# A fixed instruction sequence for every engine in a kernel that mixes a long convolution and a gated linear unit

## The chip, the cores and the metric

The kernel runs on one core of a Trainium2 chip. A core has four compute engines that run their own instruction queues strictly in order: TensorE (PE, with its weight loads shown as PEld), VectorE (DVE), ScalarE (ACT) and GpSimd (POOL). SyncE (SP) issues nearly all of this kernel's DMAs, also in order. Engines wait for each other through semaphores, so an instruction whose input is late holds up everything behind it on its own engine. The metric is the device time of one execution in microseconds; lower is better.

## What is computed

Two branches work on the same input `u` (2048 positions, 448 channels) and are mixed by a gate per position. All is in 32-bit floats. Cut to what matters:

```python
def _A_ref(u, log_A_real, A_imag, C_real, C_imag, log_dt, D_skip):
    dt = jnp.exp(log_dt)
    A = -jnp.exp(log_A_real) + 1j * A_imag            # 448 x 256
    C = (C_real + 1j * C_imag) * dt[:, None]
    P = jnp.exp((A * dt[:, None])[:, :, None] * pos[None, None, :])
    K = 2.0 * jnp.einsum("dn,dnl->dl", C, P).real     # a filter of 2048 taps per channel
    y = irfft(rfft(u_t, 2 * L) * rfft(K, 2 * L))[:, :, :L]
    return y + u * D_skip

def _B_ref(x, w_gate, w_up, w_down):
    return (sigmoid(x @ w_gate) * (x @ w_up)) @ w_down   # 448 -> 1792 -> 448

g = sigmoid((x * gate_w).sum(-1, keepdims=True))
return g * a + (1 - g) * b
```

## The kernel before

The program is written as a list of operations: each names its engine, a cost, what it reads and writes, and a priority. The class `Plan` turns the list into one order for each engine (`Plan.order`, from L457) and then emits the instructions in that order (`Plan.emit`). The order is worked out while the program is built; on the chip each engine just runs its own fixed list. To find the order, the planner keeps a clock per engine (`Clock`, L350 to L422), takes the engine that could start something first, and among the operations that could start by then picks the one with the smallest priority. The priorities are the numbers of the table `RANK`: for each kind of operation (engine, tile, stage) up to eight numbers, spread over the operations of that kind. The clock counts 450 ns for each DMA that SP issues, whatever its shape, and then 1000 ns, the transfer itself and 550 ns until it has landed.

The work falls into these parts.

- **Constants and parameters** (`step_sizes`, `params`, L926 to L1075; tiles named `..._pro`). Small VectorE chains turn the step sizes and the complex parameters of A and C into two tables in DRAM, `phd` (phases) and `bsd` (powers of the decays). `params` runs once for each half of the channels. Two constant tables are loaded by GpSimd through its own DMA queue (`cast`, L617), which rounds them on the way: `idn`, a 128x128 identity, and `pos`, 96x1024 position patterns.
- **Kernel generation** (`kgen`, 28 chunks of 16 channels, each in two halves, so 56 half chunks). GpSimd multiplies out a table of powers (`tb`, L1105 to L1118). For each half chunk PE makes two 128x512 turn tiles (`turns`, L1128), ScalarE rounds them (L1138, L1139), PE subtracts the rounded part by a matmul with the identity (L1141), ScalarE takes sine and cosine (L1143, L1144, L1158), VectorE makes outer products of the powers (L1165) and multiplies them in (L1179 to L1185), and PE contracts the result to filter taps (L1191, 64 matmuls a half chunk). ScalarE puts the taps into the tile `ke` (L1215). After 14 chunks `ke` goes to DRAM as `kd0`, after 28 as `kd1`; the last VectorE step of each is the addition at L1219.
- **Four transforms** (`Chain`): two for the halves of the input (stage 30 in the tables, stored to `us`), one for each half of the filter (stages 40 and 41). A chain loads its tile `fx`, does a first matmul stage (`stage1_four`, L716), a transposition (through DRAM as `shf`, or on VectorE), a second stage (L749); the filter chains then multiply with `us` (L783), transform back (L793, L830) and add into the output (L834). All input chains and the first filter chain use one and the same tile `fx_fu`, so the next chain's loads wait until the last chain's stores have landed.
- **The gated linear unit** (`glu_up`, `glu_down`). A product is split into rounded and remainder parts, so that a 448-long contraction takes eleven matmuls of 128x512 in four units (`glu_mm`, L1296 to L1301); the way down takes three of 128x448 a step (L1313 to L1315). There are 448 units of the first kind and 224 of the second. Rounding is done by ScalarE (L1244, L1270, L1287), remainders by VectorE (L1248 to L1251, L1272, L1288). The input tile `xs` of 512 positions is loaded and rounded in quarters: two halves of the positions times two halves of the contraction.

Of the PE's work, the gated linear unit depends on nothing but loads and rounding, and the planner spreads it between the steps of kernel generation and the transforms.

## Time and profile before

| | |
|---|---|
| median of 3 runs | 741.96 us (739.8 to 743.25) |
| the profiled execution | 740.59 us, of which the span of the trace is 738.8 us |
| granted TensorE clock, mean | 0.979 |
| kernel generation on VectorE | from 112.3 us (first L1165) to 544 us, with its end at L1219 at 557 us |
| DMAs issued by SP | 379, of which 276.9 us are spent issuing |

How to read what follows. Times in rows are microseconds from the start of the span unless marked ns. A row of the windows shows the busy time of each engine in a stretch, with the number of instructions in brackets, then the granted clock, the DMA share and GB/s. A row of the waits names who waited for whom, with the total, the number of times and the longest. In the chain of waits and the timeline a row starts with its start and its length; a bracket at the end of a timeline row is the idle time of the engine just ahead of it and what ended it. SPq is SP issuing a DMA. A matmul record is about twice as long as the distance to the next one, since matmuls overlap.

### The profile page before, as it was taken

What the parts mean: (1) busy time and instruction counts of PE and PEld (TensorE: products, weight loads), DVE (VectorE), ACT (ScalarE), POOL (GpSimd) and SP (SyncE); (2) the same over time, 40 slices, a digit from 0 to 9 for tenths busy, and PEclk for the clock granted to TensorE, in tenths of its full rate; (3) what the DMA queues carried; (4) which work ended last, traced back from release to release, by engine and by line L of the source; (5) the groups of instructions that cost most, each with busy time, mean ns of one, the idle gap of its engine ahead of it and who ended that gap; (6) DMA issues with size and microseconds to landing.
All of it is one profiled execution on the core that took longest, in us unless ns stands there. A gap on an engine that the chain in (4) does not pass through costs nothing.

```text
span 738.8 us, 16536 instructions
## 1 busy us (share of the span) xinstructions
PE 688.4 (93%) x6628; PEld 498.6 (67%) x6628; DVE 637.9 (86%) x847; ACT 523.7 (71%) x962; POOL 232.7 (32%) x282
## 2 busy tenths in 40 slices
PE   4999899999999999978998899999999899999996
PEld 3788777677757776745666677777778566445863
DVE  6999998999999979999898779999995259775976
ACT  5578749999899779998998789999882342233110
POOL 0043446563455435434543324654400000000000
PEclk9999999999999999988999899999999999999998
DMA  9658337925949945469797913239516963787975
GB/s 291 200 122 217 108 79 203 239 91 171 202 121 223 219 107 160 171 175 204 183 232 180 220 45 125 86 133 175 119 40 131 271 226 100 249 304 207 168 191 142
DMA packets 98660, 126.12 MB, mean 171 GB/s; under 512 B 31224, under 2 KB 81080, under 8 KB 97560
## 3 DMA queue, kind: packets, MB, share of 16 engines
q1 hardware_dynamic: 98328, 124.61, 65.0%
q8 instruction: 52, 0.85, 0.5%
q0 software_dynamic: 256, 0.46, 0.3%
q14 instruction: 24, 0.20, 0.1%
HBM read 81.46 MB, written 43.58 MB: 169 GB/s over the span
## 4 chain that ended last, share of the span: by engine, by line
PE 42%; DVE 19%; ACT 16%; DMA 14%; issue 5%; SPq 3%; POOL 2%; ACTq 0%; DVEq 0%
PE kp_egp L1191 4%; PE gu_gps L1296 4%; PE dn_gps L1313 4%; PE gu_gps L1297 4%; PE gu_gps L1298 4%; PE dn_gps L1314 3%; PE dn_gps L1315 3%; DMA fx_fu<-shf 3%; SPq L615 3%; DVE es_eg L1165 2%; PE tp_egp L1128 2%; PE tp_egp L1141 2%; ACT nn_eg L1139 2%; DMA us<-fx_fu 2%; PE fps_fups L716 2%
## 5 line engine op out<-in xcount | busy, mean ns | idle before, releaser
L1296 PE MATMUL gu_gps<-xs_glu,wh_glu 128*128 128x512 f32 x336 | 138.1, 411 | 16.5 <-ACT wh_glu L1270 10.1
L1298 PE MATMUL gu_gps<-xs_glu,wl_glu 128*128 128x512 f32 x336 | 133.2, 397 | 0.4 <-DVE wl_glu L1272 0.4
L1297 PE MATMUL gu_gps<-xs_glu,wh_glu 128*128 128x512 f32 x336 | 133.3, 397 | 0.0
L1165 DVE TENSOR_TENSOR es_eg<-tb_eg 128x1024 f32<-128x1024 f32 x112 | 107.4, 988 | 7.0 <-POOL tb_eg L1115 3.7
L1313 PE MATMUL dn_gps<-vh_glu,hh_glu 128*128 128x448 f32 x224 | 87.9, 393 | 2.8 <-DVE ob_glu L1329 2.6
L1296 PEld LDWEIGHTS gu_gps<-xs_glu,wh_glu 128*128 128x128 f32 x336 | 64.1, 191 | 39.2 <-ACT wh_glu L1270 10.1
L1115 POOL TENSOR_TENSOR tb_eg<-tb_eg 128x96 f32<-128x96 f32 (+2 forms) x84 | 82.2, 982 | 6.2
L1314 PE MATMUL dn_gps<-vh_glu,hl_glu 128*128 128x448 f32 x224 | 82.6, 369 | 0.6 <-issue 0.4
L1315 PE MATMUL dn_gps<-vl_glu,hh_glu 128*128 128x448 f32 x224 | 82.3, 368 | 0.0
L1139 ACT ACTIVATE nn_eg<-fr_eg 128x512 fp32r<-128x512 f32 x112 | 75.0, 669 | 10.3 <-PE tp_egp L1141 10.1
L1329 DVE SCALAR_TENSOR_TENSOR ob_glu<-dn_gps,og,ob_glu 128x448 f32<-128x448 f32 x72 | 48.7, 677 | 30.2 <-PE dn_gps L1315 30.0
L1298 PEld LDWEIGHTS gu_gps<-xs_glu,wl_glu 128*128 128x128 f32 x336 | 64.0, 191 | 15.6 <-DVE wl_glu L1272 1.1
L1297 PEld LDWEIGHTS gu_gps<-xs_glu,wh_glu 128*128 128x128 f32 x336 | 64.2, 191 | 11.4
L1105 POOL MEMSET tb_eg<- 128x96 f32 x28 | 7.8, 283 | 201.1 <-DVE es_eg L1165 200.9
L1144 ACT ACTIVATE fr_eg<-tp_egp 128x512 f32<-128x512 f32 x112 | 69.9, 629 | 0.3 <-PE tp_egp L1141 0.3
L1185 DVE TENSOR_TENSOR es_eg<-fr_eg,es_eg 128x1024 f32<-128x1024 f32 x56 | 69.8, 1246 | 0.1
L1143 ACT ACTIVATE ec_eg<-tp_egp 128x512 f32<-128x512 f32 x112 | 69.4, 625 | 0.3 <-PE tp_egp L1141 0.2
L1183 DVE TENSOR_TENSOR ec_eg<-ec_eg,es_eg 128x1024 f32<-128x1024 f32 x56 | 69.5, 1241 | 0.1
L1138 ACT ACTIVATE fr_eg<-tp_egp 128x512 f32<-128x512 f32 x112 | 64.0, 636 | 7.2 <-DVE es_eg L1185 5.1
L1158 ACT ACTIVATE ec_eg<-ec_eg,half_pi 128x1024 f32<-128x1024 f32 x56 | 67.1, 1197 | 0.1
L1118 POOL TENSOR_TENSOR tb_eg<-tb_eg,bs_eg 128x32 f32<-128x32 f32 x84 | 62.0, 741 | 6.2
L1284 ACT ACTIVATE sg_glu<-gu_gps 128x512 f32<-128x512 f32 x56 | 34.0, 608 | 37.5 <-PE gu_gps L1301 35.3
(154 smaller groups left out, 1423.0 us busy)
## 6 DMA issues: line engine op xcount, KB each, us to landing
shf<-fx_fu SPq DMA_DIRECT2D x16, 896.0 KB, 4.1
fx_fu<-shf SPq DMA_DIRECT2D x16, 896.0 KB, 15.9
us<-fx_fu SPq DMA_DIRECT2D x16, 896.0 KB, 6.7
xr_glu<-in_w_dram SPq DMA_DIRECT2D x52, 256.0 KB, 3.0
ua_fk<-us SPq DMA_DIRECT2D x16, 448.0 KB, 6.0
uax_fk<-us SPq DMA_DIRECT2D x16, 448.0 KB, 4.5
vr_glu<-in_w_dram SPq DMA_DIRECT2D x28, 224.0 KB, 5.1
gt_pre<-in_u_dram SPq DMA_DIRECT2D x8, 448.0 KB, 4.9
```

The lines of the kernel that those rows point to most:

```text
L1115: pool(96 * m, lambda n=n, m=m: G.tensor_mul(g3(n + 1, m), g3(1, m), g3(n, 1).to_broadcast([128, 32, 3, m])))
L1139: op("Act", c_act(512), lambda: S.activation(nn.real, fi(), AF.Copy, scale=-1.0, bias=MAGIC), [(fr, i)], [nn], prio)
L1144: op("Act", c_act(512, True), lambda: S.activation(fr[:, ds], tv(), AF.Sin, scale=TWO_PI), [tp], [(fr, i)], prio, table="sin")
L1165: V.tensor_mul(o.rearrange("p d (i k) -> p d i k", k=ny), x.unsqueeze(3).to_broadcast([128, 16, nx, ny]), y.unsqueeze(2).to_broadcast([128 ...
L1183: op("DVE", c_dve(1024), lambda: V.tensor_mul(ec[:, :, 32:96], ec[:, :, 32:96], es[:, :, 32:96]), [(es, 1), (es, 2)], [(ec, "p")], prio)
L1185: op("DVE", c_dve(1024), lambda: V.tensor_mul(es[:, :, 32:96], fr.real, es[:, :, 32:96]), [fr], [(es, 1), (es, 2)], prio)
L1296: T.matmul(p.real, wh[:, k, cs], x[:, k], start=(k == 0), stop=False)
L1297: T.matmul(p.real, wh[:, k, cs], x[:, 4 + k], start=False, stop=False)
L1298: T.matmul(p.real, wl[:, k, cs], x[:, k], start=False, stop=False)
L1313: T.matmul(p[:, :D], hh[:, ts], vh.real, start=(i == 0), stop=False)
L1314: T.matmul(p[:, :D], hl[:, ts], vh.real, start=False, stop=False)
L1315: T.matmul(p[:, :D], hh[:, ts], vl.real, start=False, stop=(i == len(fs) - 1))
```

## The change

The operations and their results stay the same. Five things are different.

1. `RANK` and the choice by priority are gone. A table `PLACE` gives each operation of an engine its place in that engine's list. The planner's clock is now only used to interleave the engines' lists when the instructions are emitted.
2. The planner's clock counts the time that SP takes to issue a DMA by its kind: 400 ns by default, 600 to 700 ns for several kinds, 1400 ns for a store to `us`, 3000 ns for a store to `kd`. The lead of a GpSimd instruction is 85 ns longer.
3. In the planner, a unit of `glu_mm` depends on the two quarters of `xs` that it reads and on one half of the weights, where before it depended on all of them.
4. The tables `idn` and `pos` are no longer loaded by GpSimd at the start. SP loads them as plain floats, later, in three pieces through a tile of kind `xr0`, and ScalarE rounds them (function `rounded`).
5. As a result SP issues 382 DMAs instead of 379, GpSimd none instead of two, and ScalarE has three more instructions.

The core of the diff (the table has some 200 entries, of which a few are shown):

```diff
-RANK = {
-    ('PE', 'fps', 30): (-627, 64, -344.5, -698, -438.5, -445.5, -700, 701),
...
+PLACE = {
...
+    ('DVE', 'es', 20): (162, 173, 178, 190, 176, 202, 209, 208, 210, 212, 216, 217, 218, 219, 223, 224, 226, 229, 230,
...
+    ('DVE', 'ke', 20): (434, 669,),
...
+    ('PE', 'fps', 30): (215, 222, 234, 238, 247, 253, 268, 279, 333, 339, 347, 351, 355, 361, 367, 372, 433, 440, 458,
...
+    ('PE', 'fps', 40): (681, 690, 705, 716, 723, 732, 745, 753, 826, 897, 901, 905, 908, 928, 932, 937, 939, 947, 954,
...
+    ('PE', 'fps', 41): (885, 888, 894, 896, 898, 900, 902, 904, 933, 938, 940, 946, 948, 953, 955, 961, 963, 968, 970,
...
+    ('PE', 'kp', 20): (197, 206, 217, 231, 241, 246, 255, 269, 281, 292, 305, 313, 324, 338, 350, 362, 371, 387, 394,
+        409, 424, 439, 447, 459, 477, 478, 495, 501, 516, 529, 536, 545, 556, 568, 578, 591, 602, 612, 627, 642, 656,
+        662, 680, 691, 706, 717, 724, 744, 752, 766, 776, 791, 804, 825, 837, 838,),
...
+    ('SP', 'fx', 30): (90, 92, 94, 96, 101, 107, 98, 100, 123, 121, 124, 122, 149, 153, 151, 152, 164, 155, 169, 158,
+        186, 193, 192, 191,),
+    ('SP', 'fx', 40): (226, 231, 230, 235, 239, 233, 240, 234, 258, 259, 260, 262, 333, 335, 336, 334,),
...
+    ('SP', 'kd0', 20): (190, 188, 189, 187,),
...
+    ('SP', 'ph', 20): (64, 67, 69, 78, 103, 106, 111, 117, 125, 126, 132, 137, 157, 161, 170, 172, 181, 184, 195, 197,
+        200, 208, 215, 220, 236, 238, 248, 250,),
...
+    ('SP', 'us0', 30): (135, 136, 133, 141, 142, 144, 143, 145,),
+    ('SP', 'us1', 30): (219, 206, 205, 212, 223, 222, 224, 221,),
...
+    ('SP', 'xr0', 0): (0, 1, 2, 3, 4, 5,),
...
+    ('SP', 'xr0', 10): (21, 25, 31,),
 }
...
-            self.free[e] = t + (self.ISSUE if e == "SP" else self.CAST)
+            self.free[e] = t + (o["issue"] if e == "SP" else self.CAST)
...
+        for key, places in PLACE.items():
+            for o, place in zip(kinds[key], places, strict=True):
+                o["place"] = place
...
+        queue = {e: sorted((o for o in ops if o["eng"] == e), key=lambda o: -o["place"]) for e in engines}
...
-                lo, ok = None, []
-                for o in cand[e]:
-                    t = start_of(o)
-                    if t is not None:
-                        ok.append((t, o))
-                        lo = t if lo is None else min(lo, t)
...
+                t = start_of(queue[e][-1]) if queue[e] else None
+                if t is not None:
+                    te = clock.when(e, t)
+                    if best is None or te < best[0]:
+                        best = (te, e)
...
-            o = min((o for t, o in ok if t <= te), key=rank)
-            cand[e].remove(o)
+            te, e = best
+            o = queue[e].pop()
...
 def c_pool(n):
-    return [(2.08 * n + 60.0, True, 90.0)]
+    return [(2.08 * n + 60.0, True, 175.0)]
...
-    def dma(dst, src, size, r, w, prio, rate=ROW, **kw):
+    def dma(dst, src, size, r, w, prio, rate=ROW, issue=400.0, **kw):
...
-                            64 * 16 * HD * 4, self.keys(8 * q, 8 * q + 8), [(us, (q, g, c))], prio)
+                            64 * 16 * HD * 4, self.keys(8 * q, 8 * q + 8), [(us, (q, g, c))], prio, ROW, 1400.0)
...
-                    32 * 64 * 224, [ke], [(kd[hh], j)], prio, SHORT)
+                    32 * 64 * 224, [ke], [(kd[hh], j)], prio, SHORT, 3000.0)
...
         for k in range(4):
-            op("PE", c_mm(512, 3 if k < 3 else 2), lambda k=k: g(k), [x, wh, wl], [p], pe)
+            z = 2 * (k // 2)
+            op("PE", c_mm(512, 3 if k < 3 else 2), lambda k=k: g(k), [(x, (0, z)), (x, (1, z)), (wh, z), (wl, z)], [p], pe)
...
+    def rounded(t, src, p, n, a=0):
+        xr = raw_tile(True)
+        flat = lambda: xr[:p].rearrange("p a b -> p (a b)")[:, :n]
+        dma(flat, lambda: src[:, a:a + n], p * n * 4, [], [xr], P_PRO)
+        op("Act", c_act(n), lambda: S.activation(t[:, a:a + n], flat(), AF.Copy), [xr], [(t, a)], P_PRO)
...
-    cast(lambda: idn.real, lambda: idt, 128 * 512, [], [idn], 1, 250.0)
-    cast(lambda: pos.real, lambda: post, 96 * 4096, [], [pos], P_PRO)
...
+    rounded(idn, idt, 128, 128)
...
+    for i in range(2):
+        rounded(pos, post, 96, 512, 512 * i)
```

More of the change, by code (lines that the diff above doesn't have):

```diff
@@ new lines @@
+PLACE = {
+    ('Act', 'aci', 10): (23, 52,),
+    ('Act', 'aci', 19): (91, 124,),
+    ('Act', 'acr', 10): (24, 50, 66,),
+    ('Act', 'acr', 19): (95, 121, 138,),
+    ('Act', 'ai', 10): (48,),
+    ('Act', 'ai', 19): (108,),
+    ('Act', 'bsx0', 10): (64, 69,),
+    ('Act', 'bsx0', 19): (133, 134,),
+    ('Act', 'ci', 10): (59, 70, 77,),
+    ('Act', 'ci', 19): (132, 140, 148,),
+    ('Act', 'cr', 10): (57,),
+    ('Act', 'cr', 19): (131,),
+    ('Act', 'dots', 1): (22,),
+    ('Act', 'dots', 2): (46,),
+    ('Act', 'dots', 16): (72, 86,),
[37 rows of a table added]
+    ('Act', 'idn', 10): (20,),
+    ('Act', 'junk', 10): (43, 78,),
+    ('Act', 'junk', 19): (98, 111, 155,),
[12 rows of a table added]
+    ('Act', 'pos_sb', 10): (73, 49,),
[24 rows of a table added]
+    ('DVE', 'aci', 10): (58,),
+    ('DVE', 'aci', 19): (149,),
+    ('DVE', 'acr', 10): (109,),
+    ('DVE', 'acr', 19): (188,),
+    ('DVE', 'ai', 10): (93,),
+    ('DVE', 'ai', 19): (183,),
+    ('DVE', 'bsx0', 10): (105, 133,),
+    ('DVE', 'bsx0', 19): (189, 204,),
+    ('DVE', 'ci', 10): (81,),
+    ('DVE', 'ci', 19): (175,),
+    ('DVE', 'cr', 10): (82, 85,),
+    ('DVE', 'cr', 19): (174, 180,),
+    ('DVE', 'dt2', 10): (54,),
+    ('DVE', 'dtp', 10): (45,),
+    ('DVE', 'dtv', 10): (41,),
[25 rows of a table added]
+    ('DVE', 'half_pi', 0): (49,),
[22 rows of a table added]
+    ('DVE', 'ones', 10): (32,),
[7 rows of a table added]
+    ('DVE', 'skip', 20): (37,),
[6 rows of a table added]
+    ('DVE', 'uax', 40): (691, 690, 694, 693, 706, 705, 713, 714, 723, 720, 732, 729, 739, 738, 746, 745, 769, 770,
[147 rows of a table added]
@@ L426, in pool, with op @@
         return Pool(self, name, space, after, side)
-    def op(self, eng, cost, fn, r=(), w=(), prio=0, after=(), size=0, table=None):
+    def op(self, eng, cost, fn, r=(), w=(), prio=0, after=(), size=0, table=None, issue=0.0):
         x = w[0][0] if isinstance(w[0], tuple) else w[0]
         key = eng, x.tag or x.name, prio
-        me = dict(i=len(self.ops), eng=eng, cost=cost, fn=fn, key=key, prio=prio, size=size, table=table,
+        me = dict(i=len(self.ops), eng=eng, cost=cost, fn=fn, key=key, prio=prio, size=size, table=table, issue=issue,
                   deps=set(), res=[], new=[], order=[a["i"] for a in after])
@@ L485, in start_of @@
         def start_of(o):
+            if need[o["i"]]:
+                return None
             t, n = ready[o["i"]], {}
```

88 lines of the change are left out of this document (11 added, 77 removed), and 417 rows, old and new, of tables (PLACE, RANK).

## The prediction

> **What bounds the kernel now.** I read the page's busy shares first, then the windows, cut where kernel generation begins and ends on VectorE, then the waits inside the middle window, then the chain of waits around the largest of them.
>
> ```profile
> PE 688.4 (93%) x6628; PEld 498.6 (67%) x6628; DVE 637.9 (86%) x847; ACT 523.7 (71%) x962; POOL 232.7 (32%) x282
> 0.00:112.00 112.00, 96.35 (x424) 78.88 (x425) 101.17 (x193) 74.00 (x131) 32.87 (x32) 1.00 0.62 169
> 112.00:544.00 432.00, 409.91 (x4955) 300.04 (x4953) 404.92 (x486) 394.83 (x729) 199.88 (x250) 0.97 0.66 162
> 544.00:738.80 194.80, 182.15 (x1252) 119.68 (x1251) 131.86 (x171) 54.84 (x104) 0.00 (x0) 0.98 0.69 191
> ```
>
> The page alone points at PE, but the windows show two regimes. Up to 544 us VectorE has 506.1 us of work (101.17 + 404.92) and 37.9 us of idle time; kernel generation cannot end earlier than that work allows. After 544 us VectorE is idle for a third of the time and PE is busy for 182.15 of 194.8 us: there PE and the DMA round trips of the second filter transform set the end. So a new order can win what VectorE idles before 544 us (37.9) and what PE idles after it (12.65), and no operation is made cheaper.
>
> Where does VectorE's idle time in the middle window (432 - 404.92 = 27.1 us) come from?
>
> ```profile
> DVE ec_eg L1179 <- ACT ec_eg L1158: 9.8, 7, 4.1
> DVE ob_glu L1329 <- PE dn_gps L1315: 4.1, 2, 3.2
> DVE es_eg L1165 <- POOL tb_eg L1115: 3.7, 3, 2.4
> DVE vl_glu L1272 <- ACT vh_glu L1270: 2.0, 2, 1.6
> ```
>
> The names are those of the last link only. The chain of waits shows the start of it, at two places:
>
> ```profile
> 235.87 2.11 SPq L615
> 238.03 16.29 DMA us<-fx_fu
> 255.13 5.15 DMA fx_fu<-in_u_dram
> 260.32 1.72 PE fps_fups L716 x6
> ...
> 415.44 5.74 DMA fx_fu<-kd
> 421.21 1.86 PE fps_fups L716 x6
> ...
> 263.92 0.68 DVE L1329 SCALAR_TENSOR_TENSOR ob_glu<-dn_gps,og,ob_glu 128x448 f32<-128x448 f32 x1 [3.15 <-PE dn_gps L1315]
> 267.28 0.69 DVE L1179 TENSOR_TENSOR ec_eg<-ec_eg,es_eg 128x512 f32<-128x512 f32 x1 [0.94 <-ACT ec_eg L1158]
> ...
> 423.99 0.69 DVE L1179 TENSOR_TENSOR ec_eg<-ec_eg,es_eg 128x512 f32<-128x512 f32 x1 [4.10 <-ACT ec_eg L1158]
> 428.28 1.83 DVE L1165 TENSOR_TENSOR es_eg<-tb_eg 128x1024 f32<-128x1024 f32 x2 [0.60 <-PE kp_egp L1191]
> 432.54 1.93 DVE L1165 TENSOR_TENSOR es_eg<-tb_eg 128x1024 f32<-128x1024 f32 x2 [2.43 <-POOL tb_eg L1115]
> 439.56 0.69 DVE L1288 TENSOR_TENSOR hl_glu<-sg_glu,hh_glu 128x512 fp32r<-128x512 f32 x1 [0.95 <-ACT hh_glu L1287]
> ```
>
> Both times a transform's first matmul (L716) stood at the head of PE's queue before its load had landed. The turn matmuls behind it waited too, then ScalarE, then VectorE: 3.15 + 0.94 = 4.1 us, and 4.10 + 0.60 + 2.43 + 0.95 = 8.1 us. That is 12.2 of the 27.1 us. The rest is spread over small waits.
>
> **The change part by part.** The sum is made against the profiled execution, 740.59 us (span 738.8 and 1.8 around it); the median of the runs, 741.96, is 1.4 above it, and I carry the difference over.
>
> *Where the order moves the two stalls.* How far PE had come when those matmuls were reached is counted by kernel generation's own matmuls, 64 a half chunk:
>
> ```profile
> 112.00:257.90 145.90, 19.00 (x1088) 16.09 (x1088) 1.00 0.75 184
> 112.00:418.00 306.00, 43.43 (x2368) 36.72 (x2368) 0.97 0.74 182
> 112.00:544.00 432.00, 61.59 (x3392) 52.29 (x3392) 0.97 0.66 162
> L615 SPq DMA_DIRECT2D us<-fx_fu x16: 313/994/2638, 215.1 to 398.1; - x16
> L615 SPq DMA_DIRECT2D kd<-ke_eg x8: 619/2700/3444, 350.8 to 563.2; - x8
> ```
>
> 1088/64 = 17 and 2368/64 = 37 half chunks. In the new list of PE the same two matmuls have places 433 and 681, behind the half chunks with places 424 and 680, which are the 21st and 43rd: four and six later. A half chunk takes 432 x 64/3392 = 8.2 us, so they come 33 and 49 us later. The loads do not move as far. The second input chain's first load (SP place 149) still stands between the `ph` loads of chunks 11 and 12; the filter chain's (226) falls behind those of chunks 22 and 23, which can only be issued once chunk 19 has freed their buffer, so at most two chunks or 33 us later than before. That leaves 33 and at least 16 us of new slack against waits of 2.5 us at most. The planner's reason is visible in the last two rows: a store to `kd` holds SP for 2.7 us and one to `us` for 1.0, where it used to count 0.45. I take both stalls as gone, less 1 us for what opens elsewhere: **-11 us**. Bounds: -19 (only 8 of 27.1 us of idle time left) and +6 (the slower rival below).
>
> [...] The rows:
>
> ```profile
> 330.00:335.00 5.00, 3.49 (x51) 2.00 (x51) 4.97 (x7) 4.66 (x9) 0.00 (x0) 0.50 1.15 197
> 420.00:425.00 5.00, 3.79 (x11) 2.94 (x12) 0.98 (x2) 2.07 (x3) 0.00 (x0) 0.59 1.10 208
> PE fps_fups L716 <- DMA fx_fu<-kd: 2.8, 2, 2.5
> ```
>
> The granted clock was 0.50 and 0.59 where PE was idle for 1.5 and 1.2 us of five. The longest wait of PE in the middle window is 2.5 us. [...] I leave this out of the sum and make it a rival.
>
> *The quarters.* Does a matmul on the chip wait for less than before?
>
> ```profile
> 9.97 0.42 DVE L1250 TENSOR_TENSOR xs_glu<-xr_pre,xs_glu 128x256 fp32r<-128x256 f32 x1
> 10.08 0.80 PE L1296 MATMUL gu_gps<-xs_glu,wh_glu 128*128 128x512 f32 x1 [10.08 <-ACT wh_glu L1270]
> 10.41 0.42 DVE L1251 TENSOR_TENSOR xs_glu<-xr_pre,xs_glu 64x256 fp32r<-64x256 f32 x1
> ```
>
> The first matmul started at 10.08 us while VectorE was still writing the last quarter of `xs` (to 10.83). So the chip already waits by parts; this edit alters only what the planner may put first, and by itself is worth nothing.
>
> *The start.* SP now sends the six first loads without another between them, and `idn` and `pos` come later.
>
> ```profile
> 1.26 0.71 POOL L618 DMA_DIRECT2D pos_sb<-in_post_dram  x1 [0.81 <-POOLq L1433]
> 1.97 0.55 POOL L618 DMA_DIRECT2D idn<-in_idt_dram  x1
> 7.60 1.80 ACT L1244 ACTIVATE xs_glu<-xr_pre 128x512 fp32r<-128x512 f32 x3 [3.47 <-DMA xr_pre<-in_ut_dram]
> 0.00:20.00 20.00, 9.54 (x33) 7.34 (x34) 12.66 (x42) 12.16 (x20) 1.46 (x6) 1.00 0.98 293
> ```
>
> The two tables are 448 KB; at 293 GB/s that is 1.6 us of a DMA share of 0.98, which the first quarters no longer wait behind. Against it, VectorE's new list begins with the roundings of `xs`, so the step-size chain (20 instructions of about 0.16 us, 3.2 us) no longer fills part of the idle 7.34 us but falls into busy time. The three new issues on SP take about 0.4 us each. ScalarE's three roundings are bounded by the 0.63 us of a 512-wide one, 1.9 us in all, beside 38 us of idle time before 112 us; if that cover were gone they would cost those 1.9 us. Between -4 (all early idle time halved) and +3 (the chain exposed), I take **-1 us**. [...]
>
> Kernel generation also opens earlier: its first L1165 has place 162, which with four two-instruction roundings ahead is the 167th instruction, where before 193 ended by 112 us. Its last step `ke` has place 669, and before some 679 instructions had run by 544 us: the same work, counted with the doubled ones. The 26 instructions (26 x 101.17/193 = 14 us) of the second half's parameters are only moved in among kernel generation. POOL does the same with its part of them; POOL is busy for 200 of 432 us. Nothing in the sum.
>
> *The tail.* From the last half chunk to the first transform matmul on `kd1`:
>
> ```profile
> 556.30:579.90 23.60, 23.60 (x108) 20.05 (x108) 10.52 (x18) 7.57 (x13) 0.00 (x0) 1.00 0.75 189
> 583.87 0.46 PE L716 MATMUL fps_fkps<-fx_fk,ft_fk 64*128 64x224 f32 x2 [3.29 <-DMA fx_fk<-kd]
> PEld fps_fups L793 <- issue: 6.0, 25, 0.4
> ```
>
> 108 matmuls cover that stretch; the new list has 46 units there (places 839 to 884), 30 of the first kind and 16 of the second, or 30 x 2.75 + 16 x 3 = 131 matmuls. The 23 more, at 23.6/108 = 0.22 us, are 5 us: the wait of 3.3 us goes. After the last half chunk PE changes between the unit's matmuls and the transforms' 59 times instead of 75; at 6.0/25 = 0.24 us of weight-load idle time, partly hidden, 16 fewer are worth 0 to 4 us, I take 0.7. **-4 us**, between -8 and +5 (a load late again).
>
> Sum: -1 - 11 - 4 = -16: 724.6 for such an execution, 726 as a median. Moved DMAs, SP's total issue time but for 1.2 us, and ScalarE's and POOL's work are unchanged, and I price them at nothing else.
>
> **The rivals.**
>
> *The stalls move (same).* The planner still counts 1.55 us and the transfer for a load to land, 2.7 us for one of `fx`, where the rows above have 5.15 and 5.74. Heads of queues may wait at new places for as long. For it: a list that is packed tighter against a wrong latency. Against it: the counted slack of 16 and 33 us. Then 27.1 us of idle time stay 25: 740.
>
> *The turn pairs are too close (slower).* Between a turn matmul (L1128) and the identity matmul (L1141) of its pair, PE had 4.0 us of other work on average by the old list and has 3.2 by the new.
>
> ```profile
> L1139 ACT ACTIVATE nn_eg<-fr_eg 128x512 fp32r<-128x512 f32 x110 | 73.7, 670 | 10.3 <-PE tp_egp L1141 10.1
> PE tp_egp L1141 <- ACT nn_eg L1139: 8.1, 9, 1.9
> ```
>
> ScalarE needs 0.64 + 0.67 us for the pair and serves other work between. Nine of 110 pairs now wait, 8.1 us in all. If half of the pairs waited 0.5 us more, that is 28 us on a PE that has 22 idle in this window: the stage grows by 6 and the kept gain is nil, 748. It decides from 22/110 = 0.2 us more a pair. Against it: 3.2 us is still twice the two activations.
>
> *The clock comes back (faster still).* With no stall, the half-clock stretches go too, and the small waits with them: middle window -19, tail -6, start -1: 716.
>
> **How the numbers follow.** Chances: the forecast (720 to 736) 0.55, the clock rival 0.14, same 0.16, slower 0.15. Half a per cent, about what a measurement of this kernel can tell from no change, is 3.7 us. Faster 0.69, same 0.16, slower 0.15. The range 711 to 744 has the lower ends of all three terms (-31) at the bottom, takes in the unchanged case, and leaves out most of the slower one.
>
> **What would show it.** Right: PE's L716 no longer waits over 1 us for `fx_fu`, VectorE idles under 18 us in a middle window that ends with the last half chunk near 530 us, and no L716 wait on `fx_fk`. Wrong: waits at L1141 grow past 20 us, a load of `ph` or `xr` late behind a blocked SP, or VectorE's work itself grows since POOL now runs beside other instructions. The time is wrong if VectorE's idle time before the last half chunk stays near 38 us.

## The result, and the profile after

The changed kernel takes 714.94 us (median of 4 runs, 713.72 to 720.98) against 742.49 us before (4 runs, 739.80 to 743.25). The ratio is 0.9642, with a 95% interval of 0.9604 to 0.9681: 27.5 us less, where the forecast had 16. The forecast was 726 us with a range of 711 to 744; the time lies in the range, near its fast end, and close to the 716 us of the rival "the clock comes back". The profiled execution took 715.01 us with a span of 713.2.

One number of the record has to be corrected first. The table of before and the prediction say that kernel generation opens on VectorE at 112.3 us. The source view of that line (shortest, median and longest duration in ns, first and last start) shows 123.7 us before:

```profile
L1165 DVE TENSOR_TENSOR es_eg<-tb_eg x112: 673/1207/1855, 123.7 to 548.6; 128x1024 f32<-128x1024 f32 x56, 128x512 f32<-128x512 f32 x56
```

The same view of the changed kernel shows 102.3 us:

```profile
L1265 DVE TENSOR_TENSOR es_eg<-tb_eg x112: 677/990/1917, 102.3 to 531.0; 128x1024 f32<-128x1024 f32 x56, 128x512 f32<-128x512 f32 x56
```

(Lines of the body moved by 100.) Its last start, 548.6 us before, is also later than the 544 of that table. The windows of the prediction were cut at 112 and 544 us, which are not the same point of the work in both kernels. Below they are cut at the first contraction matmul (L1191, L1291) of the first and of the last half chunk, which are. Columns: PE, PEld, DVE, ACT and POOL busy, then the granted clock, DMA share and GB/s. The windows of before:

```profile
0.00:134.80 134.80, 118.55 (x526) 95.99 (x529) 122.02 (x221) 95.31 (x170) 49.70 (x54) 1.00 0.66 177
134.80:555.10 420.30, 397.76 (x5015) 290.21 (x5013) 395.17 (x471) 381.02 (x704) 183.04 (x229) 0.97 0.63 156
555.10:738.80 183.70, 172.09 (x1094) 112.40 (x1093) 120.76 (x157) 47.34 (x90) 0.00 (x0) 0.98 0.72 200
```

The windows of the changed kernel at the same three points:

```profile
0.00:131.30 131.30, 121.99 (x541) 101.11 (x541) 117.89 (x224) 97.51 (x171) 43.85 (x46) 1.00 0.60 160
131.30:537.60 406.30, 388.57 (x5001) 284.30 (x5004) 388.90 (x469) 384.54 (x707) 188.68 (x234) 0.98 0.67 168
537.60:713.20 175.60, 167.44 (x1103) 110.29 (x1091) 121.28 (x157) 46.63 (x90) 0.00 (x0) 0.99 0.75 211
```

The opening is 3.5 us shorter, kernel generation 14.0, the tail 8.1: 25.6 us of span, where the forecast had 1, 11 and 4. What PE waits for in the whole span (total in us, times, longest), from the waits of before:

```profile
PE gu_gps L1296 <- ACT wh_glu L1270: 10.1, 1, 10.1
PE tp_egp L1141 <- ACT nn_eg L1139: 8.3, 10, 1.9
PE gu_gps L1296 <- ACT sg_glu L1284: 4.2, 5, 2.0
PE fps_fkps L716 <- DMA fx_fk<-kd: 3.3, 1, 3.3
PE fps_fups L716 <- DMA fx_fu<-kd: 2.8, 2, 2.5
PE dn_gps L1313 <- DVE ob_glu L1329: 2.6, 5, 0.8
...
PE fps_fups L716 <- DMA fx_fu<-in_u_dram: 2.4, 2, 1.8
```

The same view of the changed kernel:

```profile
PE gu_gps L1396 <- ACT wh_glu L1370: 8.2, 1, 8.2
PE kp_egp L1291 <- issue: 5.3, 2, 3.1
PE tp_egp L1241 <- ACT nn_eg L1239: 4.5, 9, 1.2
PE dn_gps L1414 <- DVE ob_glu L1430: 4.1, 5, 1.6
...
PE fps_fups L816 <- DMA ft_fu<-in_s1t_dram: 0.5, 1, 0.5
```

The three rows of waits for a transform's load (`in_u`, `kd` into `fx_fu`, `kd` into `fx_fk`) are gone in this execution, the waits inside turn pairs have fallen by almost half, and a new one has come, "issue" at L1291, to which the last section returns. The page of the changed kernel, busy times and chain:

```profile
PE 678.0 (95%) x6628; PEld 495.7 (70%) x6628; DVE 628.1 (88%) x847; ACT 528.7 (74%) x967; POOL 232.5 (33%) x280
PE 59%; ACT 24%; DMA 6%; DVE 6%; issue 3%; SPq 1%; ACTq 0%; DVEq 0%
```

The second line is the chain that ended last, by engine. Before, it read:

```profile
PE 42%; DVE 19%; ACT 16%; DMA 14%; issue 5%; SPq 3%; POOL 2%; ACTq 0%; DVEq 0%
```

VectorE has gone from 19% of the chain to 6%, DMA and SP from 17% to 7%; PE from 42% to 59%, and ScalarE from 16% to 24%.

**A ledger of PE.** The same three numbers can be taken from every page: the span, PE's busy time and the mean granted clock. Idle is span minus busy. "Lost" is (1 - clock) x span, the time that the half clock can at most have cost. What is left of the busy time is PE's work at full clock.

| kernel | span | PE idle | lost to the clock | PE's work at full clock |
|---|---|---|---|---|
| before | 738.8 | 50.4 | 15.5 | 672.9 |
| after | 713.2 | 35.2 | 8.6 | 669.4 |

Of the 25.6 us, 15.2 are idle time of PE and 6.9 the clock; 3.5 are left. The sum holds by construction, for PE as for any other engine: a span is busy time plus idle time. So the ledger shows where the time went and not what caused it; for that there are the experiments.

### The profile page after: what moved, and what is told of

It reads as the page before. It is cut to its first block, busy times and chain, and to the rows that moved or that the text cites. A ratio compares the mean times of both kernels' runs of the same rounds, so it can differ in the third digit from the quotient of the medians.

```text
span 713.2 us, 16520 instructions
## 1 busy us (share of the span) xinstructions
PE 678.0 (95%) x6628; PEld 495.7 (70%) x6628; DVE 628.1 (88%) x847; ACT 528.7 (74%) x967; POOL 232.5 (33%) x280
## 4 chain that ended last, share of the span: by engine, by line
PE 59%; ACT 24%; DMA 6%; DVE 6%; issue 3%; SPq 1%; ACTq 0%; DVEq 0%
PE gu_gps L1396 7%; PE gu_gps L1397 7%; PE gu_gps L1398 7%; PE dn_gps L1414 6%; PE dn_gps L1415 5%; PE dn_gps L1416 5%; PE kp_egp L1291 4%; ACT nn_eg L1239 4%; ACT ec_eg L1243 3%; ACT fr_eg L1238 3%; PE tp_egp L1241 3%; ACT fr_eg L1244 3%; ACT ec_eg L1258 3%; DMA fx_fu<-shf 3%; PE gu_gps L1400 2%
## 5 line engine op out<-in xcount | busy, mean ns | idle before, releaser
L1396 PE MATMUL gu_gps<-xs_glu,wh_glu 128*128 128x512 f32 x336 | 136.4, 406 | 11.5 <-ACT wh_glu L1370 8.2
L1265 DVE TENSOR_TENSOR es_eg<-tb_eg 128x1024 f32<-128x1024 f32 (+1 forms) x112 | 109.0, 991 | 4.8 <-PE kp_egp L1291 3.8
L1215 POOL TENSOR_TENSOR tb_eg<-tb_eg 128x96 f32<-128x96 f32 (+2 forms) x84 | 89.3, 1063 | 6.2
L1238 ACT ACTIVATE fr_eg<-tp_egp 128x512 f32<-128x512 f32 x112 | 70.3, 636 | 10.6 <-PE tp_egp L1228 8.0
L1285 DVE TENSOR_TENSOR es_eg<-fr_eg,es_eg 128x1024 f32<-128x1024 f32 x56 | 72.0, 1286 | 0.7
L1244 ACT ACTIVATE fr_eg<-tp_egp 128x512 f32<-128x512 f32 x112 | 69.7, 633 | 0.1
L1414 PEld LDWEIGHTS dn_gps<-vh_glu,hh_glu 128*128 128x128 f32 x224 | 42.7, 191 | 26.6 <-DVE ob_glu L1430 10.8
```

The source lines that it names most:

```text
L1215: pool(96 * m, lambda n=n, m=m: G.tensor_mul(g3(n + 1, m), g3(1, m), g3(n, 1).to_broadcast([128, 32, 3, m])))
L1238: op("Act", c_act(512, True), lambda: S.activation(fi(), tp.real, AF.Copy, bias=MAGIC), [tp], [(fr, i)], prio)
L1244: op("Act", c_act(512, True), lambda: S.activation(fr[:, ds], tv(), AF.Sin, scale=TWO_PI), [tp], [(fr, i)], prio, table="sin")
L1265: V.tensor_mul(o.rearrange("p d (i k) -> p d i k", k=ny), x.unsqueeze(3).to_broadcast([128, 16, nx, ny]), y.unsqueeze(2).to_broadcast([128 ...
L1396: T.matmul(p.real, wh[:, k, cs], x[:, k], start=(k == 0), stop=False)
L1414: T.matmul(p[:, :D], hh[:, ts], vh.real, start=(i == 0), stop=False)
```

## The experiments

All of them reorder or thin out one of the two kernels; line numbers differ a little between them, the tiles' names do not. "Old" and "new" are the orders before and after the change. A ratio is to runs of the kernel before that were made beside it; their medians lie between 741.0 and 744.1 us, so differences of 2 or 3 us between kernels of different experiments are better taken from the ratios.

**1 and 2. Which part of the order pays?** The lists were cut at the second addition into `ke` on VectorE, the end of kernel generation. One kernel runs the new order up to there and the old one behind it, the other the reverse.

```diff
 each engine's list, up to and with the last step DVE ke.20[1]
-old order
+new order                 (h1; in h2 the other way round)
 each engine's list, behind it: what is left, in the
 old order                 (h1; in h2 the new one)
```

> The new order up to the last addition of kernel generation (the second ke step), from there every engine takes what is left in the order of before. The traces put 17.4 us of the gain ahead of the last half chunk (556.2 to 538.8) and 8.2 behind it (182.6 to 174.4). Theory A, the order of the tail earns its 8 us itself: 723 us (721 to 726). Rival, the tail is only shorter because it starts from a better state and without half clock: 715 to 717.

> The order of before, with its tables loaded by GpSimd, up to the last addition of kernel generation, then what is left in the new order. Theory A: 734 us (732 to 736), 8 us less than before. Rival: 740 to 742.

New head, old tail: 727.33 us (723.93 to 729.97), ratio 0.9777 [0.9727, 0.9828]. Old head, new tail: 736.46 us, ratio 0.9896 [0.9853, 0.9939]. So the head brings some 16 us and the tail some 7, and together they make most of the 27. Both times lie a little above what Theory A gave (721 to 726, 732 to 736), and away from the rivals. In the first, the tail's wait came back, and longer:

```profile
PE fps_fkps L703 <- DMA fx_fk<-kd: 5.5, 1, 5.5
```

**3 and 4. Is the opening worth nothing, as the prediction had it?** The same cut, ahead of the first L1165 on VectorE.

```diff
 each engine's list, ahead of the first step DVE es.20[0]
-new order
+old order                 (h3; in h4 the other way round)
 each engine's list, behind it: what is left, in the
 new order                 (h3; in h4 the old one)
```

> The order of before, tables by GpSimd, up to the first product of kernel generation on VectorE (L1165 of before, at 123.7 us there and 102.3 in the new trace), then what is left in the new order. By the prediction's step (VectorE's work ahead of the end of kernel generation is the same, so an earlier opening is worth nothing in itself): 715 to 719 us, kernel generation ending within 4 us of the new one. Rival, the opening is where the gain ahead of the tail was made, since in the old opening VectorE's parameter steps stand beside GpSimd's and get longer: 727 to 733.

> The new order up to the first product of kernel generation on VectorE, then what is left in the order of before. By the prediction's step: 738 to 742 us, since the two late transform loads stand where they stood. Rival, the opening made the gain: 724 to 731.

The old opening with the new order behind it took 731.77 us, ratio 0.9837 [0.9793, 0.9881], so 17 us more than the changed kernel and in the rival's range; its first contraction matmul came at 147.9 us, and from there it ran as the changed kernel does (windows at the same three points):

```profile
0.00:147.90 147.90, 127.88 (x544) 102.35 (x544) 125.06 (x227) 95.80 (x168) 43.89 (x48) 0.98 0.61 160
147.90:553.50 405.60, 387.15 (x5005) 281.90 (x5008) 386.85 (x465) 383.88 (x705) 186.93 (x234) 0.99 0.65 161
553.50:729.20 175.70, 167.28 (x1099) 110.47 (x1087) 121.14 (x157) 46.65 (x90) 0.00 (x0) 1.00 0.76 210
```

The new opening with the old order behind it took 744.04 us, ratio 1.0002 [0.9971, 1.0033]: in this form it is worth nothing. Its first contraction matmul came at 138.1 us, later than before's 134.8. Both kernels have a seam, at which one list's remaining parameter steps meet the other's; in the second, PE waits 6.3 us there (waits of that kernel):

```profile
PE fps_fups L1058 <- ACT cr_pro L935: 6.3, 1, 6.3
```

So neither of the two prices the opening by itself. What they show is that it is not free to exchange, which the prediction's "nothing in the sum" took for granted.

**5 and 6. Does VectorE set the pace of kernel generation?** The prediction says so, and VectorE's work up to the last `ke` step did fall, by 10 us. Some of VectorE's instructions take longer with GpSimd's products beside them (804 against 688 ns for one group, shown in the last section). The two kernels leave out GpSimd's power products in kernel generation and fill the tile of powers with a constant, in the new order and in the old.

```diff
-        pool(96, lambda: G.memset(g3(0, 1), 1.0), lambda n: [(0.5 * n, False, 0.0)])
+        pool(96, lambda: G.memset(tb.real, 1.0), lambda n: [(0.5 * n, False, 0.0)])
...
-            pool(96 * m, lambda n=n, m=m: G.tensor_mul(g3(n + 1, m), g3(1, m), g3(n, 1).to_broadcast([128, 32, 3, m])))
+            pool(96 * m, lambda: None)
...
-            pool(32, lambda e=e: G.tensor_mul(t(e + 1), t(e), b(3)))
+            pool(32, lambda: None)
```

> The changed kernel without GpSimd's power products in kernel generation (the 84 first squarings and the 84 products with the table of bases, 143.8 us of GpSimd's time); the tile of powers is filled once with a constant, so the output is not the reference's. All else keeps its order. Theory A (VectorE's SBUF-only instructions are stretched by a GpSimd instruction beside them, and this is what the new order wins a part of): VectorE's work before its last ke addition falls from 508.6 us to 485-495, most of it in L1265 and the other instructions that read no PSUM, those that read PSUM keep their durations, and the time is 698-706. Rival B (GpSimd is hidden, the shorter work of VectorE in the changed kernel has another cause): VectorE's work stays within 3 us of 508.6 and the time is 713-717. Rival C (the stretch is real but PE sets the pace of kernel generation): VectorE's work falls as in A, its idle time takes it up, time 710-717.

> The order of before without GpSimd's power products in kernel generation, as in the run with the new order: the 84 squarings and 84 products are left out and the tile of powers holds a constant, so the output is not the reference's. Theory A (in the old order VectorE sets the pace of kernel generation, as the prediction has it: relieved of the stretch by GpSimd it ends earlier by most of that): VectorE's work before its last ke addition falls by 15-22 us from 518.5, and the time is 724-732. Rival B (PE's waits and its clock set the pace there too, as the run with the new order showed for that one): VectorE's work falls as much, its idle time takes it up, and the time is 736-741.

New order: 714.30 us, ratio 0.9636 [0.9594, 0.9679], no different from the changed kernel's 0.9642. Old order: 742.26 us, ratio 1.0023 [1.0000, 1.0047], no faster than before. In both, VectorE was relieved as expected. The third busy time of a window is VectorE's. The window up to the last `ke` step in the kernel before:

```profile
0.00:557.00 557.00, 518.22 (x5603) 387.95 (x5604) 518.53 (x694) 477.58 (x874) 232.75 (x282) 0.98 0.64 160
```

In the old order without the products:

```profile
0.00:558.90 558.90, 520.62 (x5603) 389.58 (x5604) 497.81 (x693) 476.96 (x874) 92.39 (x114) 0.98 0.64 160
```

In the changed kernel:

```profile
0.00:540.00 540.00, 512.96 (x5611) 387.57 (x5612) 508.50 (x693) 483.23 (x879) 232.53 (x280) 0.99 0.65 165
```

In the new order without the products:

```profile
0.00:537.60 537.60, 508.73 (x5611) 385.21 (x5612) 492.74 (x693) 482.61 (x879) 93.97 (x112) 0.99 0.66 166
```

VectorE's work falls by 20.7 us in the old order and by 15.8 in the new one, and the end of kernel generation moves by +1.9 and by -2.4 us. VectorE's idle time takes up nearly everything. Rival C of the new order's run and Rival B of the old order's are what happened (the second with a time 1 us above its 736 to 741): relieving VectorE moves the end in neither order, although it is busy for 93% of that window before. That PE sets the pace instead is argued and not shown, since no run takes work from PE. Experiment 10 speaks for it. ScalarE, busy for 483 us of the 540 and a larger part of the chain than before, is a rival that was not tried.

**7, 8 and 9. Are the two stalls worth 11 us?** They were the prediction's main term. These kernels keep the old order and move only the matmuls that stood at the head of PE's queue ahead of their loads, with the ScalarE steps that empty their results.

```diff
 old order, PE's list (c1)
-388: fps.30[16]   617: fps.40[0]
+396: fps.30[16]   624: fps.40[0]
 old order, ScalarE's list (c1)
-365: fx.30[32]  371: fx.30[33]  637: fx.40[0]
+373: fx.30[32]  374: fx.30[33]  645: fx.40[0]
 c2: as c1, and in PE's list
-397: fps.30[17]
+406: fps.30[17]
 c3: the moves of fps.40[0] and fx.40[0] alone
```

> The order of before, in which only the two matmuls that stood at the head of PE's queue ahead of their loads are moved eight and seven places later (the first of the second input chain, with the two ScalarE moves out of its result; the first of the first filter chain, with one of them). Everything else stands as before the change. Theory A (the prediction's main term: the two stalls and what queues up behind them cost about 11 us, and with them goes the half clock that follows each): no wait over 1 us on fx_fu<-in_u or fx_fu<-kd, full clock at 260 and 421 us, time 727-732 against 742. Rival B (VectorE is nearly full from 310 to 355 us and catches up with most of it; only PE's own waits of 5.2 us can be won): 735-738. Rival C (both waits are slack that other engines fill): 740 or more.

> The order of before, in which only the first matmul of the first filter chain (the one that waited 2.5 us at 421 us) is moved seven places later, with the one ScalarE move that empties its result; the second input chain stands as before the change. Theory A (PE sets the pace: a stall costs PE's own wait and the half clock after it, 2.5 + 3.4 us, and nothing takes it back): no half clock near 420 us, the stretch from the 32nd to the 40th half chunk falls from 68.4 us to about 63, and the time is 734-737. Rival B (what is won there is given back at the next tight place before kernel generation ends): the stretch is shorter, but the last half chunk begins within 2 us of before's 555.1 us and the time is 739.5 or more.

> As the run with both heads moved, but the second unit of the second input chain is moved as well, so that it does not follow the first at once and wait for its result to be emptied. Theory A (PE sets the pace; the two stalls cost their waits of 2.4 + 2.8 us and the half clock after them, 1.7 + 3.4 us): no wait over 1 us at the two places, and the time is 730-734. Rival B (won and given back before the end, or at the same tight stretch of 310 to 355 us): 738 or more.

| kernel | median | ratio to before | 95% interval |
|---|---|---|---|
| c1, both heads | 740.49 | 0.9979 | 0.9954 to 1.0004 |
| c3, filter chain's head alone | 740.57 | 0.9971 | 0.9949 to 0.9993 |
| c2, both, and the second unit | 741.82 | 0.9977 | 0.9958 to 0.9996 |

Between 0.2 and 0.3%, some 2 us, where Theory A expected 5 to 15: the last rival's time in all three. The traces of c1 and c2 show where it went. In c1 PE no longer waited for the input load, but for ScalarE to empty the moved matmul's result, since the chain's second unit followed at once (waits of c1):

```profile
PE fps_fups L705 <- ACT fx_fu L708: 2.1, 1, 2.1
```

In c2, which puts that right, the waits for both loads are gone, and those inside the turn pairs have grown from 8.3 us (L1141 before) to 12.8 (waits of c2):

```profile
PE tp_egp L1130 <- ACT nn_eg L1128: 12.8, 13, 3.2
```

The longest of them in c2's timeline:

```profile
278.11 0.50 PE L1130 MATMUL tp_egp<-nn_eg,idn 128*128 128x512 f32 x1 [3.21 <-ACT nn_eg L1128]
```

The units that now stand ahead of the load are missing a few microseconds later, where they had covered ScalarE's rounding. The second stall was a better bargain. From the 31st half chunk to the last, the window of before:

```profile
368.70:555.10 186.40, 178.68 (x2266) 133.55 (x2265) 173.83 (x206) 167.80 (x309) 76.25 (x93) 0.98 0.54 134
```

The same stretch in c2:

```profile
373.20:554.10 180.90, 175.97 (x2270) 130.97 (x2269) 174.18 (x207) 167.47 (x309) 78.72 (x94) 1.00 0.55 138
```

And in c3:

```profile
371.90:554.30 182.40, 176.05 (x2266) 131.13 (x2265) 174.57 (x206) 167.50 (x309) 78.55 (x93) 1.00 0.56 137
```

That stretch is 5.5 us shorter in c2 and 4.0 in c3. In c2 it is 2.8 us less idle time of PE, and 2.7 us less busy time for nearly the same matmuls, with the clock at 1.00 instead of 0.98. It is what Theory A counts for that stall, 2.5 us of wait and at most 3.4 of half clock (before, the granted clock was 0.50 for 6.8 us from 420.9 us on). But the stretch ahead of it, from the first to the 31st half chunk, is 1.8 us longer in c3's profile, where nothing was moved (371.9 less a first start at 136.2, against 368.7 - 134.8), and 3.8 in c2's (from 135.5). By the ratios the whole gains only some 2 us; how much of the difference is the scatter of single executions stays open.

**10. And a stall put back in?** The new order, with only the first matmul of the second input chain moved ahead of 13 units (the expectation counts 14 places), to a place that its load does not reach in time.

```diff
 new order, PE's list
-433: fps.30[16]
+420: fps.30[16]
```

> The changed kernel, with only the first transform matmul of the second input chain moved 14 places earlier in PE's list, to where its load has not landed (about 271 us; the load is issued at 272 and has landed some 8 to 9 us later). Theory A (a load that is late at the head of PE's queue holds up the turn matmuls, then ScalarE, then VectorE, and the end of kernel generation moves by nearly all of it): one wait of 7-9 us at L816 on fx_fu<-in_u, VectorE idle 5-9 us more before ke, time 720-724 against 715 for the changed kernel. Rival B (what is buffered between PE and VectorE, and the slack of a kernel that is not bound there, hides it): the wait is seen, but the time is within 2 us of 715.

726.44 us (724.46 to 727.17), ratio 0.9794 [0.9756, 0.9831]: 11.5 us more than the changed kernel, and above the 720 to 724 of Theory A, whose mechanism it shows. The waits:

```profile
PE fps_fups L703 <- DMA fx_fu<-in_u_dram: 6.0, 2, 3.2
```

The windows in which it waits and resumes:

```profile
275.00:280.00 5.00, 0.98 (x2) 0.40 (x2) 5.00 (x7) 2.11 (x4) 4.26 (x6) 0.79 0.83 187
280.00:285.00 5.00, 3.43 (x10) 2.52 (x11) 0.66 (x1) 0.00 (x0) 0.00 (x0) 0.50 0.46 105
```

Six microseconds of waiting, then half clock (0.79, 0.50), and VectorE, which worked through the wait (5.00 of 5), idle after it. Kernel generation is 7.8 us longer than in the changed kernel (133.3 to 547.4 us, so 414.1 against 406.3), and VectorE idles 7.2 us more in it, inside Theory A's 5 to 9. The whole difference is idle time of PE (25.5 against 17.7); the clock took no more than in the changed kernel (0.99 against 0.98), whose profile has its half clock behind other stops. The other 4.2 us of the span fall into the opening and the tail, where nothing was moved. So the late head cost its own wait of 6.0 us and some 2 us of further idle time; the half clock behind it does not show in the sum.

**11. The two tables.** The new order, with `idn` and `pos` loaded and rounded by GpSimd at the start as before.

```diff
+    cast(lambda: idn.real, lambda: idt, 128 * 512, [], [idn], 1, 250.0)
+    cast(lambda: pos.real, lambda: post, 96 * 4096, [], [pos], P_PRO)
...
-    rounded(idn, idt, 128, 128)
...
-    for i in range(2):
-        rounded(pos, post, 96, 512, 512 * i)
```

> The changed kernel, with only the two constant tables loaded and rounded by GpSimd's own queue at the start, as before the change (the new order of everything else is kept, the three loads by SP and ScalarE's three roundings of them fall away). Theory A (the tables' 448 KB delay the first input quarters by their transfer alone): the first matmul starts near 10 us instead of 8.2 and the time is 716-718. Rival B (the later tables bring nothing by themselves, the opening has idle time enough): 714-715.5. Rival C (the tables were the larger part of the earlier opening): 719 or more.

719.05 us (715.73 to 721.21), ratio 0.9698 [0.9644, 0.9751]: about 4 us more than the changed kernel by the medians, with intervals that overlap. The first matmul started at 9.9 us, where in six kernels with the later tables (the changed one and experiments 1, 4, 5, 10 and 12) it started at 8.2 to 9.2, and in the eight with GpSimd's tables at 9.3 to 10.3. So about a microsecond is shown at its place; the rest is not resolved. The median is 1 us above Theory A's 716 to 718 and just reaches the 719 of Rival C, and the runs cover both.

**12. The tail's head.** The new order, with the first matmul of the second filter chain 7 places earlier.

```diff
 new order, PE's list
-885: fps.41[0]
+878: fps.41[0]
```

> The changed kernel, with only the first transform matmul of the second filter chain moved 7 units earlier in PE's list, towards its place in the old tail. The filler in front of it is then some 20 matmuls or 4.5 us shorter. Theory A (in the tail PE and the round trips of the second filter transform set the end, and the filler ahead of that matmul must cover the landing of the store to kd1 and of the load): a wait of 1-4 us at L816 on fx_fk<-kd appears, and the time is 716-719. Rival B (the store and load have landed well before, the place is slack): no such wait and 714-715.5.

717.05 us (715.53 to 718.94), ratio 0.9673 [0.9635, 0.9711], 2 us more than the changed kernel, inside Theory A's 716 to 719 but not resolved from no change. The wait that Theory A asked for was not there: no wait at L703 on `fx_fk<-kd`. So seven places of filler there are slack, and the theory of a tight cover falls in this form; the wait of 5.5 us in the first experiment is that of the whole old tail. PE waited 2.0 us elsewhere in this profile, for the first filter chain's load (`fx_fu<-kd`), ahead of anything that was moved.

**All runs in PE's ledger.**

| kernel | span | PE idle | lost to the clock | PE's work at full clock | mean clock of all timed runs |
|---|---|---|---|---|---|
| before | 738.8 | 50.4 | 15.5 | 672.9 | 0.976 to 0.978 (60 runs) |
| after | 713.2 | 35.2 | 8.6 | 669.4 | 0.991 (4) |
| 1: new head, old tail | 723.6 | 44.7 | 6.5 | 672.4 | 0.988 (4) |
| 2: old head, new tail | 731.6 | 46.7 | 11.7 | 673.2 | 0.981 (4) |
| 3: old opening | 729.2 | 46.9 | 7.3 | 675.0 | 0.990 (4) |
| 4: new opening | 744.5 | 53.2 | 20.8 | 670.5 | 0.973 (10) |
| 5: new, no products | 710.6 | 36.9 | 5.0 | 668.7 | 0.992 (4) |
| 6: old, no products | 743.1 | 50.5 | 18.6 | 674.0 | 0.976 (10) |
| 7: old, both heads (c1) | 739.2 | 48.4 | 17.0 | 673.8 | 0.979 (10) |
| 8: old, filter head (c3) | 737.7 | 48.2 | 15.5 | 674.0 | 0.978 (11) |
| 9: old, heads apart (c2) | 740.3 | 50.2 | 15.5 | 674.6 | 0.979 (11) |
| 10: input head early | 725.2 | 46.3 | 6.5 | 672.4 | 0.989 (4) |
| 11: tables early | 716.3 | 41.1 | 2.9 | 672.3 | 0.993 (4) |
| 12: tail head early | 714.9 | 38.7 | 4.3 | 671.9 | 0.993 (4) |

PE's work at full clock stays between 669 and 675 us in fourteen kernels whose spans differ by 34 us, and whose VectorE work differs by 28. The matmuls are the same 6628, so that is no surprise; what the table adds is where the differences of the spans lie, in PE's idle time and in its clock. The clock follows the order of the middle: every kernel with the old one lost 11 us or more in its profile, every kernel with the new one 9 or less. The column is an upper bound, since part of the half clock falls into idle time.

## Why the prediction came out as it did

**What was right.** The direction, the range, and the list of places. In the changed kernel's profile PE no longer waits over 1 us for `fx_fu` (0.5 us is left, on a table's load), the tail's wait on `fx_fk` is gone, and VectorE idles 17.4 us (406.30 - 388.90) in kernel generation, under the 18 that were named as the sign. The window ends at 537.6 us; "near 530" was 14 less than the 544 of its window, so about 541 at this landmark. The queue that the prediction worried about did not appear: the turn pairs' waits fell from 8.3 to 4.5 us, so the slower rival is refuted for this order (c2 shows that it lives next door). The "same" rival, stalls that only move, is what c1 and c2 did; in the new order it happened in part, as the slack below shows.

**The step that failed: "kernel generation cannot end earlier than that work allows", with VectorE as the engine whose idle time counts.** As a bound it is true, but it was not what held, and its work was no constant: of the 14.0 us that kernel generation became shorter, VectorE's idle time gave 7.7 (25.1 to 17.4) and its shorter work 6.3 (395.17 to 388.90), which the prediction held fixed. Relieving VectorE of 21 us in the old order gained nothing. The prediction read 506 us of work in 544 and concluded that VectorE sets the pace; a share of 93% is not a pace. The windows had the hint: in kernel generation PE was busy for 397.76 of 420.30 us and VectorE for 395.17, no less, and the busy shares alone cannot say which of the two waits for the other.

**The step "I take both stalls as gone", -11.** Kernel generation gained 14.0 us, so the term was about right in size, but not for its reasons. The slack of "33 and at least 16 us" is not there. A half chunk takes 7.6 us (420.3/55) and not 8.2, since none ran in the first 23 us of the prediction's window; the new order starts earlier and runs faster; and the loads moved nearly as far as the matmuls. The second input chain's first load is issued 17.8 us later than before (254.40), and its first matmul starts 22.1 us later (257.93). The changed kernel's rows, from SP's and PE's timelines:

```profile
272.19 0.65 SPq L717 DMA_DIRECT2D fx_fu<-in_u_dram  x1
280.01 1.57 PE L816 MATMUL fps_fups<-fx_fu,ft_fu 64*128 64x224 f32 x8
```

For the first filter chain it is 21.3 us (414.11 to 435.37) against 27.0 (418.06 to 445.03). So the new order wins 4 and 6 us of lead over waits of 2.4 and 2.8. The matmuls stand close behind their loads, and in five of the other six kernels with the new middle PE waits for the filter chain's load again, for 0.7 to 2.2 us; the longest is in experiment 5 (PE's timeline there):

```profile
443.08 1.02 PE L703 MATMUL fps_fups<-fx_fu,ft_fu 64*128 64x224 f32 x6 [2.24 <-DMA fx_fu<-kd]
```

That is nearly the 2.5 us of before, in a kernel of 714.30 us. Moved by themselves in the old order the same two matmuls bring 2 us; in c2 the units put in front of one wait were missing at another. The price of a stall was summed over VectorE's idle time (12.2 us), where PE itself had waited 5.2, and it left out the clock. In the changed kernel's profile kernel generation has 4.8 us less idle time of PE (22.5 to 17.7) and some 4.5 us less lost to the clock (420.30 x 0.03 against 406.30 x 0.02, clocks rounded to two places). The other 4.7 us go with work that moved: in the opening PE is busy for 3.4 us more in 3.5 us less.

**The term "the start", -1, and "nothing in the sum" for the opening.** Mis-sized: PE's idle time there fell by 6.9 us (16.25 to 9.3). Of these, 1.9 are the first matmul (10.1 to 8.2 us), which the prediction saw; the others are waits of the gated unit on ScalarE's sigmoid and VectorE's additions, which the prediction did not look at (waits of PE in before's opening, up to 134.8 us):

```profile
PE gu_gps L1296 <- ACT sg_glu L1284: 3.7, 4, 2.0
PE dn_gps L1313 <- DVE ob_glu L1329: 1.5, 3, 0.6
```

Neither is left in the changed kernel's opening. Experiments 3 and 4 do not price this gain, since each pays for its seam; with the old order behind it, it was not kept.

**The tail, -4.** The mechanism was right: 23 more matmuls cover the load of `kd1`, and the wait of 3.3 us went. It was 8.1 us: 3.4 of idle time, and 4.65 of busy time for almost the same matmuls. Half clock followed that wait too, but the granted clock (0.98 of 183.7 us, 0.99 of 175.6) accounts for at most some 2 of the 4.65; that the rest is PE changing between kinds of matmul less often, as the prediction has it, was not tested.

**The clock.** This is the mechanism that the forecast left out and kept as a rival, with a chance of 0.14. Both stalls of before, with waits of 2.4 and 2.8 us, had half clock behind them. PE's timeline of before around the first stall (start, length, then the matmul; the distance between starts is what a matmul costs):

```profile
256.48 0.36 PE L1313 MATMUL dn_gps<-vh_glu,hh_glu 128*128 128x448 f32 x1
256.68 0.37 PE L1314 MATMUL dn_gps<-vh_glu,hl_glu 128*128 128x448 f32 x1
...
260.32 1.72 PE L716 MATMUL fps_fups<-fx_fu,ft_fu 64*128 64x224 f32 x6 [1.75 <-DMA fx_fu<-in_u_dram]
...
262.56 0.57 PE L1313 MATMUL dn_gps<-vh_glu,hh_glu 128*128 128x448 f32 x1
262.93 0.57 PE L1314 MATMUL dn_gps<-vh_glu,hl_glu 128*128 128x448 f32 x1
```

Ahead of the wait these matmuls start 0.20 us apart, behind it 0.37, at a granted clock of 0.50 (from 260.5 us on, for 3.4 us), and the wait was 2.4 us in two parts. The second stall has its half clock in the window from 420 us that the prediction quotes (0.59), the tail's here:

```profile
584.00:589.00 5.00, 5.00 (x21) 3.04 (x22) 0.00 (x0) 1.69 (x4) 0.00 (x0) 0.66 1.12 233
```

Experiment 10 put in a stall and got half clock behind it (0.50). How much idle time it takes can be read from the clock records of the fourteen traces. In each of them the times between two changes of the clock are multiples of 3.41 us. Of 2832 such steps at full clock, all 32 in which PE idled 1.78 us or more were followed by a step at half clock, of the 84 with 1.2 to 1.77 us 24, and of the 2716 with less one (the ends of matmuls are modelled, so the bounds are rough). So the half clock behind a wait is partly luck: experiment 5's wait of 2.24 us fell across two steps, and the clock stayed at 1.00. In these traces idle time of about half of one step, 1.78 of 3.41 us, was enough every time.

Over all timed runs the clock is 0.977 before and 0.991 after, or at most 17 and 6.4 us lost: up to 10 of the 27.5 us.

**Not tried.** The waits by quarters alone, and the planner's issue times alone: they enter only through the order that was found with them, so no run of one order prices them. SP's issuing, priced as unchanged but for 1.2 us, took 287.8 us against 276.9; no run prices that either.

## What to carry to other kernels

When several engines are busy over 90%, take away work from the one that you think is the bound before you count its idle time as a gain: here VectorE at 93% could be relieved of 21 us for nothing. A stall at the head of an in-order queue can cost its own wait and half clock behind it (in experiment 10 a wait of 6.0 us, then a clock of 0.50), but its price shows only when it is taken out alone: two stalls of 5.2 us together were worth some 2 us, and in one case the filler put in front of one wait was missing at another. Parts of this change were worth 0, 7 and 16 us, and the whole 27; why they are not worth the same alone is argued from that case and not shown in general.

## What was not expected of the hardware

**PE stopped in the middle of a group of matmuls with no wait of the program.** The changed kernel's two "issue" waits of 5.3 us are these (the first is the larger one), from PE's timeline:

```profile
355.69 0.55 PE L1291 MATMUL kp_egp<-es_eg 128*32 128x64 f32 x25
359.34 0.44 PE L1291 MATMUL kp_egp<-es_eg 128*32 128x64 f32 x7 [3.10 <-issue]
```

The windows around it:

```profile
355.00:360.00 5.00, 1.90 (x67) 1.41 (x66) 5.00 (x7) 2.38 (x6) 1.47 (x2) 0.80 0.97 187
360.00:365.00 5.00, 5.00 (x14) 4.17 (x14) 2.84 (x4) 2.65 (x6) 1.86 (x5) 0.51 0.37 110
```

25 of a group's 32 matmuls had run; the other seven needed nothing new. In that gap a packet of 16 KB of the kind "instruction" moved on the DMA engines, which were then busy for 0.97 of the time. The clock fell to 0.51 behind it and VectorE lost 4.3 us. The stop recurs in the same group, 6 to 8 matmuls before its end, in every kernel with the new middle (3.1 to 3.4 us). With the old middle one kernel, experiment 2, has such a stop of 3.0 us, at another place. That PE had run out of instructions is an inference, which the traces bear out: in all fourteen traces PE has 24 stops over 0.4 us that the profile puts down to "issue", and each of them ended 1.3 to 1.8 us after the end of such a packet (by chance one in some 28 would). Why the packet came late is open: of 52 most cost nothing, and so did one at 338.2 us, with a DMA share of 1.14 around it. With 5.3 us, "issue" is PE's largest kind of wait that is left in the changed kernel behind its first matmul.

**VectorE beside GpSimd.** Two groups of instructions in the kernel before (busy us and mean ns behind the bar), one that reads two SBUF tiles, and one that reads PSUM:

```profile
L1179 DVE TENSOR_TENSOR ec_eg<-ec_eg,es_eg 128x512 f32<-128x512 f32 x56 | 45.0, 804 | 10.2 <-ACT ec_eg L1158 9.8
...
L1285 DVE SCALAR_TENSOR_TENSOR sg_glu<-sg_glu,gu_gps 128x512 f32<-128x512 f32 x56 | 38.0, 679 | 9.6 <-PE gu_gps L1301 7.7 <-ACT sg_glu L1284 1.3 <-ACT hh_glu L1287 0.4
```

The same two in the old order without the power products:

```profile
L1168 DVE TENSOR_TENSOR ec_eg<-ec_eg,es_eg 128x512 f32<-128x512 f32 x56 | 38.5, 688 | 16.3 <-ACT ec_eg L1147 15.9
L1274 DVE SCALAR_TENSOR_TENSOR sg_glu<-sg_glu,gu_gps 128x512 f32<-128x512 f32 x56 | 38.3, 684 | 15.9 <-PE gu_gps L1290 13.5 <-ACT sg_glu L1273 1.3 <-ACT hh_glu L1276 0.4
```

804 against 688 ns for the first, 679 against 684 for the second: the first is longer with GpSimd's products beside it, the second is not. Why that is so was not shown. The changed order has less of it in this group (717 ns), and by experiments 5 and 6 that is not where its time came from.
